# A gated attention mix on one core: the maxima task of row block 0 moves from the last A group of a slot into the second group of the next slot

## The chip, the cores and the metric

The kernel runs on one core of one Trainium2 chip. The metric is the time of one execution on the device, in microseconds (us). The time before is the median of three executions.

Engine names in the rows: PE is the matmul engine (TensorE) and PEld its weight loads, DVE is VectorE, ACT is ScalarE, POOL is GpSimd, and SP is the engine that issues most DMAs.

## The reference

One input `x` (2048 x 512) goes through two attention blocks with 32 heads of 16 dimensions. Block A is causal within each of four segments of 512 rows, and mixes in a running memory state per head; block B is full attention over 2048 rows. A gate per row mixes the two.

```python
def _A_ref(x, wq, wk, wv, wo, beta):          # H = 32, Dh = 16, N = 4 segments, L = 512
    ...
    for s in range(N):
        logits = einsum("bhqd,bhkd->bhqk", qs, ks) * scale + mask     # causal inside the segment
        p = _softmax(logits, axis=-1)
        a_dot = einsum("bhqk,bhkd->bhqd", p, vs)
        ...                                                           # a_mem from the state of the segments before
        o = g * a_mem + (1.0 - g) * a_dot
    return o @ wo

def _B_ref(x, wqkv, wo):
    scores = einsum("bhqd,bhkd->bhqk", q, k) * (Dh ** -0.5)
    p = _softmax(scores, axis=-1)
    return einsum("bhqk,bhkd->bhqd", p, v) @ wo

g = _sigmoid((x * gate_w).sum(-1, keepdims=True))
return g * _A_ref(...) + (1 - g) * _B_ref(...)
```

## The kernel before

The work of a unit is four heads and 512 query rows. There are 32 units of block A (numbered 0 to 31) and 32 of block B (32 to 63). After a first part with the projections, the main loop has 32 slots; slot k computes B's unit `ub` = 32 + k and A's unit `ua` = k.

**Two passes over the scores.** The softmax needs the row maxima before the exponentials. The first pass computes scores with the queries on the partitions and reduces them on VectorE: `s_b` (L467) is one such maxima task of B, two matmuls into a pair of PSUM banks and one reduction of 128 x 1024; `s_a` (L442) is one of A, with causal masks added by small matmuls from `crows` and `cmask`. The pairs of banks, `SBK[0]` and `SBK[1]`, take turns in the order in which the tasks are issued. `m_chain` (L480) makes the negated maxima out of both units' results, and `m_rows` (L503) puts them as extra rows into the query tiles, so that the second pass yields scores less their maximum. A's maxima of unit u go into the chain u + 1, which `m_chain` takes in group 21 of slot u.

**Groups.** The second pass computes the scores transposed, in groups. A slot has 37 groups: 32 for B and then 5 for A. `t_group` (L522) issues the two halves of a group's score matmuls into two of three banks (`tb0`, `tb1`, `mb`); between the two halves it runs the tasks that the plan gives to that group (`between`), for groups of A behind them. ScalarE then writes the exponentials into `raw`. In A's groups GpSimd cuts them to the causal triangle (L546).

**Probability times value.** `pv` (L549) accumulates the product with the values, with a column of ones for the sum, in the bank `PVB`. `pvs` (L866) sets which product comes with which group: group 0 has A's last key block of the slot before, followed by `fin_copy` (L562), in which VectorE copies `PVB` out; group 1 has none; from group 2 on come B's; A's last group has its key blocks 1 and 3.

**The plan.** All is issued in an order written out by hand; each engine takes its instructions in that order. `plan` maps (slot, group) to a list of tasks. B's maxima tasks are spread one to a group. A's six, in the order `ST_A` = (3, 0), (3, 1), (2, 0), (2, 1), (1, None), (0, None), go to the five A groups of the slot before the one that uses them: row block 3 in two halves in the first two, both halves of row block 2 in the third, row block 1 in the fourth, and row block 0 in the fifth, A's last group.

From slot 9 to slot 31, `extras` (L888) puts one output matmul block of 12 matmuls (`out_mm`, L625) ahead of group 2, in group 1.

Of the kernel before, what the change touches and what calls it, by code (L numbers as in the profile page):

```python
# [23 lines left out]
NT = SEQ // 128  # L24
# [10 lines left out]
def gated_mix_kernel(ctx, tc, xt, wq, wk, wv, wo, beta, wqkv, wob, gate_w, out):  # L35
# [635 lines left out]
    def todo(fn, *a):  # L671
        return lambda: fn(*a)
# [90 lines left out]
    for blk in range(16):  # L763
# [9 lines left out]
        n = blk + 1 + (c == 2)  # L773
# [156 lines left out]
    plan = {}  # L930

    def spread(tasks, gs):
        for n, p in enumerate(gs):
            plan.setdefault(p, []).extend(tasks[len(tasks) * n // len(gs):len(tasks) * (n + 1) // len(gs)])

    for k in range(31):
        if k:
            spread([todo(s_b, 33 + k, *t) for t in (sorted(ST_B, key=lambda t: t[2]) if k == 1 else ST_B)],
                   [(k - 1, n) for n in range(2 * S_FIRST, 2 * NT)] + [(k, n) for n in range(2 * S_LAST)])
        else:  # L940
            spread(st33[EARLY:], sorted([(0, n) for n in range(2 * S_LAST)] + [(0, 2 * n) for n in range(4)]))
        for n, t in enumerate(ST_A):
            plan.setdefault((k, 2 * NT + n - (n > 2)), []).append(todo(s_a, k + 1, *t))

    for k in range(32):
        ua, ub = k, 32 + k
# [89 lines left out]
```

## Time and profile before

| | |
|---|---|
| median of three runs | 1942.11 us (1941.66 to 2304.19) |
| the profiled execution | 1943.65 us, span 1941.9 us |
| busy: PE, DVE, ACT, POOL | 99%, 83%, 74%, 16% of the span |
| mean granted TensorE clock | 0.997 |
| slots 1, 2, 4, 5 | about 47.4 us each |
| slots 9 to 29 | about 49.4 us each |

The span reaches from the first to the last instruction; the execution's time has 1.75 us around it. In the rows of a timeline the first number is the start and the second the duration, in us; then come the engine, the line, the operation, output and inputs with their sizes, and the number of instructions merged in the row. In brackets stands the idle time of the engine before it and what ended it. The end of a matmul is modelled, so two matmuls that follow each other can overlap in the rows. Rows that group instructions give count, busy time, mean ns of one, and the idle time before them.

### The profile page before, as it was taken

The page shows a single profiled execution, that of the slowest core. Times are in us where ns is not written, and L with a number is a line of the kernel's source. Part 1 is how long each engine was busy: PE and PEld are TensorE (multiplying, and loading weights), DVE is VectorE, ACT ScalarE, POOL GpSimd, SP SyncE. Part 2 cuts the span into 40 slices and gives each one's busy share as a digit, 9 for nine tenths or more (in the row PEclk, how much of TensorE's full clock was granted, in tenths as well). Part 3 has the DMA queues.
Part 4 walks back from the last instruction along what each step waited for, and adds up shares of the span by engine and source line. Part 5 has one row for each costly group of instructions (what it writes and reads, how often), then busy time and mean ns, then how long its engine had stood idle before and what let it go on. Part 6 is the DMA issues. An engine that isn't in the chain of part 4 may idle for free.

```text
span 1941.9 us, 43661 instructions
## 1 busy us (share of the span) xinstructions
PE 1918.9 (99%) x17485; PEld 927.4 (48%) x17485; DVE 1619.4 (83%) x1678; ACT 1434.8 (74%) x2699; POOL 317.4 (16%) x665
## 2 busy tenths in 40 slices
PE   7999999999999999999999999999999999999999
PEld 5887777444344444444444444444444444444445
DVE  6135766899999999999999999999999999999942
ACT  4233333688888888888888888888888888888884
POOL 5200000011211111111121212121112121212122
PEclk9999999999999999999999999999999999999999
DMA  7666566744443444453435354544445443434111
GB/s 216 165 203 189 188 197 178 174 99 116 99 116 90 105 88 105 87 116 88 115 86 115 87 115 88 116 88 106 94 93 111 93 106 89 106 88 110 49 49 58
DMA packets 163791, 222.50 MB, mean 115 GB/s; under 512 B 39916, under 2 KB 90556, under 8 KB 157828
## 3 DMA queue, kind: packets, MB, share of 16 engines
q1 hardware_dynamic: 159284, 211.41, 44.0%
q0 software_dynamic: 3248, 8.03, 2.2%
q8 instruction: 138, 2.26, 0.5%
q14 instruction: 65, 0.53, 0.1%
q10 hardware_dynamic: 1056, 0.26, 0.1%
HBM read 147.95 MB, written 68.16 MB: 111 GB/s over the span
## 4 chain that ended last, share of the span: by engine, by line
PE 96%; DVE 2%; DMA 0%; ACT 0%; SPq 0%; issue 0%; DVEq 0%; ACTq 0%
PE pvb L559 33%; PE tb L537 18%; PE sbk L474 12%; PE mb L537 9%; PE tb L304 5%; PE sbk L452 3%; PE tb L629 2%; PE mb L304 2%; PE sbk L287 1%; PE tb L287 1%; PE pvb L304 1%; PE mb L629 1%; PE sbk L456 1%; PE mb L287 1%; PE pvb L287 1%; DVE mxb L476 1%
## 5 line engine op out<-in xcount | busy, mean ns | idle before, releaser
L476 DVE TENSOR_REDUCE mxb<-sbk 128x2 f32<-128x1024 f32 x1024 | 1233.2, 1221 | 61.5 <-PE tb L537 30.6
L543 ACT ACTIVATE raw<-tb 128x512 f32<-128x512 f32 x1555 | 887.6, 598 | 146.0 <-PE tb L537 101.8
L559 PE MATMUL pvb<-raw,vb 128*17 128x256 f32 (+1 forms) x8072 | 639.9, 388 | 0.0
L543 ACT ACTIVATE raw<-mb 128x512 f32<-128x512 f32 x782 | 467.6, 598 | 71.2 <-PE mb L537 44.9
L474 PE MATMUL sbk<-xh,qb 64*128 64x512 f32 x1344 | 479.8, 445 | 3.8 <-DVE mxb L476 1.8
L537 PE MATMUL tb<-qb,xh 64*128 64x512 f32 x872 | 352.2, 443 | 0.0
L559 PEld LDWEIGHTS pvb<-raw,vb 128*17 128x17 f32 x8072 | 134.9, 95 | 341.3 <-issue 335.9
L474 PE MATMUL sbk<-kb,qb 64*128 64x512 f32 x704 | 242.1, 444 | 0.0
L537 PEld LDWEIGHTS tb<-qb,xh 64*128 64x128 f32 x872 | 145.9, 185 | 176.6 <-issue 89.7
L537 PE MATMUL mb<-qb,xh 64*128 64x512 f32 x445 | 198.9, 447 | 0.0
L474 PEld LDWEIGHTS sbk<-xh,qb 64*128 64x128 f32 x1344 | 192.2, 184 | 9.1 <-DVE mxb L476 6.1
L537 PE MATMUL tb<-qb,kb 64*128 64x512 f32 x470 | 191.1, 447 | 0.8 <-DVE st L314 0.8
L546 POOL TENSOR_SCALAR_AFFINE_SELECT raw<-raw 128x256 f32<-128x256 f32 (+1 forms) x320 | 115.8, 362 | 355.9 <-ACT raw L543 348.2
L460 DVE TENSOR_REDUCE mx<-sbk 128x2 f32<-128x768 f32 (+1 forms) x128 | 136.6, 1090 | 23.8 <-PE sbk L456 21.1
L537 PEld LDWEIGHTS mb<-qb,xh 64*128 64x128 f32 x445 | 82.1, 184 | 94.9 <-issue 50.4
L537 PEld LDWEIGHTS tb<-qb,kb 64*128 64x128 f32 x470 | 79.2, 184 | 98.8 <-issue 53.1
L537 PE MATMUL mb<-qb,kb 64*128 64x512 f32 x234 | 104.0, 444 | 0.0
L474 PEld LDWEIGHTS sbk<-kb,qb 64*128 64x128 f32 x704 | 96.8, 184 | 5.2 <-issue 3.5
L559 PE MATMUL pvb<-raw,va 128*17 128x256 f32 (+2 forms) x1280 | 94.7, 384 | 0.8 <-ACT pvs L568 0.8
L452 PE MATMUL sbk<-ka,qa 64*128 64x256 f32 (+3 forms) x512 | 87.9, 358 | 1.3 <-DVE mx L460 0.3
L311 ACT ACTIVATE st<-tb 128x512 fp32r<-128x512 f32 x33 | 19.8, 598 | 81.4 <-DVE phi L310 47.3
L537 PE MATMUL tb<-qa,ka 64*128 64x512 f32 (+3 forms) x339 | 79.5, 372 | 0.0
(291 smaller groups left out, 1832.1 us busy)
## 6 DMA issues: line engine op xcount, KB each, us to landing
xh<-dB SPq DMA_DIRECT2D x38, 512.0 KB
vb<-vdB SPq DMA_DIRECT2D x16, 1088.0 KB
dB<-st SPq DMA_DIRECT2D x64, 256.0 KB
dA<-st SPq DMA_DIRECT2D x64, 256.0 KB
pd<-pvs SPq DMA_DIRECT2D x64, 256.0 KB
kb<-dB SPq DMA_DIRECT2D x22, 512.0 KB
xh<-dB SPq DMA_DIRECT2D x38, 256.0 KB
qb<-dB SPq DMA_DIRECT2D x64, 128.0 KB
```

The source lines that it names most:

```text
L287: nc.tensor.matmul(b, lhs, WV[wi][:, k, :], start=n == 0, stop=n == 11)
L304: nc.tensor.matmul(b, WS[ws][w][wi][:, k, :], (XH, XL)[xi][c][:, k, :], start=n == 0, stop=n == 11)
L311: nc.scalar.activation(st[:, 0], b, AF.Copy)
L452: nc.tensor.matmul(b[:, j, c0:c0 + n], q_of(u)[r, p, i * 128:(i + 1) * 128], k_of(u, p)[r, :n], start=True, stop=False)
L460: nc.vector.tensor_reduce(m[:, :, p, i], b[:, :, :n], axis=AX.X, op=OP.max)
L474: nc.tensor.matmul(b[:, j], q_of(u)[r, p, i * 128:(i + 1) * 128], k_of(u, p)[r, kc * C:(kc + 1) * C], start=True, stop=True)
L476: nc.vector.tensor_reduce(MXB[u][:, :, p, i, kc], b, axis=AX.X, op=OP.max)
L537: nc.tensor.matmul(bs[j][:, c0:c0 + w], k_of(u, h // 2)[r, 128 * it:128 * it + 128], q_of(u)[r, h // 2, q0:], start=True, stop=True)
L543: nc.scalar.activation(pt, bs[j], AF.Exp, scale=SCALE)
L546: nc.gpsimd.affine_select(out=m, in_=m, pattern=[[1, 128]] if n < 2 else [[0, 2], [1, 128]], compare_op=OP.is_ge, fill=0.0, base=0, channe ...
L559: nc.tensor.matmul(PVB[32 * h:32 * h + E + 1, q0 + lo:q0 + hi], vt[:, it, 4 * q + h, :], pt[:, lo:hi], start=it == 0 and lo == 0, stop=it ...
L629: nc.tensor.matmul(b, (AT["oh"], AT["ol"])[oi][:, g, a], (AT["wh"], AT["wl"])[wi][:, g, a], start=n == 0, stop=n == 11)
```

## The change

For slots k = 2 to 7 the sixth task of `ST_A`, row block 0 of unit k + 1 (both pairs of heads), is no longer planned for A's last group of slot k, (k, 36), but for group 1 of slot k + 1. There it stands ahead of B's maxima task of that group, and both are issued between the two halves of the group's scores. The task itself, its operands and the chain that takes its result are the same. Slots 1, 2 and 9 to 31 keep the old place.

```diff
         for n, t in enumerate(ST_A):
-            plan.setdefault((k, 2 * NT + n - (n > 2)), []).append(todo(s_a, k + 1, *t))
+            over = n == 5 and 2 <= k < 8
+            plan.setdefault((k + 1, 1) if over else (k, 2 * NT + n - (n > 2)), []).append(todo(s_a, k + 1, *t))
```

## The prediction

> **What bounds the kernel now.** I read the busy shares first, then the busy time by slot, then one slot boundary engine by engine in order of time.
>
> ```profile
> PE 1918.9 (99%) x17485; PEld 927.4 (48%) x17485; DVE 1619.4 (83%) x1678; ACT 1434.8 (74%) x2699; POOL 317.4 (16%) x665
> 451.05:498.49 47.44, 47.40 (x496) 19.10 (x493) 45.71 (x47) 40.77 (x76) 9.90 (x17) 1.00 0.51 120
> 498.49:547.08 48.59, 47.76 (x498) 19.19 (x494) 46.81 (x47) 40.87 (x76) 7.40 (x15) 1.00 0.42 100
> 547.08:594.49 47.41, 47.38 (x497) 19.14 (x493) 45.68 (x47) 40.77 (x76) 9.91 (x17) 1.00 0.49 117
> 689.56:736.94 47.38, 47.34 (x498) 19.19 (x494) 45.42 (x44) 40.72 (x76) 4.58 (x15) 1.00 0.43 90
> 736.94:784.20 47.26, 47.23 (x496) 19.16 (x492) 45.20 (x42) 40.70 (x77) 7.87 (x20) 1.00 0.50 110
> ```
>
> The first row is the page's; the others are slots 2, 3, 4, 7 and 8 (from:to and length, then busy us of PE, PEld, DVE, ACT, POOL, then the TensorE clock). TensorE is busy in all but some hundredths of a slot, at the full clock, and VectorE in 45.2 to 46.8 of 47.3 to 48.6 us. So TensorE sets the pace and VectorE, 4% below it, is the next to do so. But a modelled busy PE also covers matmuls that run without the partner they normally overlap. That shows only in order of time. The boundary into slot 3, PE alone:
>
> ```profile
> 496.72 0.50 PE L537 MATMUL tb<-qa,ka 64*128 64x256 f32 x4
> 497.06 0.22 PE L452 MATMUL sbk<-ka,qa 64*128 64x128 f32 x2
> ...
> 497.50 1.06 PE L559 MATMUL pvb<-raw,va 128*17 128x384 f32 x16
> 498.49 0.49 PE L537 MATMUL mb<-qb,kb 64*128 64x512 f32 x1
> ...
> 499.15 0.63 PE L559 MATMUL pvb<-raw,va 128*17 128x256 f32 x8
> 499.71 0.50 PE L537 MATMUL tb<-qb,kb 64*128 64x512 f32 x1
> ...
> 500.28 0.40 PE L537 MATMUL tb<-qb,kb 64*128 64x512 f32 x1
> 500.54 0.51 PE L474 MATMUL sbk<-xh,qb 64*128 64x512 f32 x2
> 500.95 0.49 PE L537 MATMUL tb<-qb,kb 64*128 64x512 f32 x1
> 501.37 0.67 PE L559 MATMUL pvb<-raw,vb 128*17 128x256 f32 x8
> 501.98 0.50 PE L537 MATMUL mb<-qb,kb 64*128 64x512 f32 x1
> 502.27 0.50 PE L474 MATMUL sbk<-xh,qb 64*128 64x512 f32 x2
> 502.61 0.39 PE L537 MATMUL tb<-qb,kb 64*128 64x512 f32 x1
> 502.93 0.63 PE L559 MATMUL pvb<-raw,vb 128*17 128x256 f32 x8
> 503.49 0.49 PE L537 MATMUL tb<-qb,kb 64*128 64x512 f32 x1
> ...
> 504.71 0.50 PE L537 MATMUL tb<-qb,kb 64*128 64x512 f32 x1
> ```
>
> Here 496.72 starts A's last group, 498.49 group 0 of slot 3, 499.71 group 1, 500.28 group 2, 501.98 group 3, 503.49 group 4, 504.71 group 5. An undisturbed group takes 1.22 us (503.49 to 504.71). Group 1 has no probability-value step and takes 0.57. Groups 2 and 3 take 1.70 and 1.51: together 0.77 us over the pace. VectorE and GpSimd in the same stretch:
>
> ```profile
> 496.28 2.03 DVE L462 TENSOR_REDUCE mx<-sbk 128x4 f32<-128x1024 f32 x2 [0.23 <-PE sbk L456]
> 499.26 1.23 DVE L476 TENSOR_REDUCE mxb<-sbk 128x2 f32<-128x1024 f32 x1 [0.94 <-PE tb L537]
> 500.40 0.68 DVE L566 COPY pvs<-pvb 128x512 f32<-128x512 f32 x1
> 501.00 4.61 DVE L476 TENSOR_REDUCE mxb<-sbk 128x2 f32<-128x1024 f32 x4
> 496.47 0.90 POOL L546 TENSOR_SCALAR_AFFINE_SELECT raw<-raw 128x256 f32<-128x256 f32 x2 [0.77 <-ACT raw L543]
> ```
>
> The reduction of group 0 ends at 499.26 + 1.23 = 500.49, and the maxima matmuls of group 2, which reuse its pair of banks, start 0.05 later, at 500.54. Group 1's reduction starts at 501.00, behind the copy of the finished output, ends at 501.00 + 1.22 = 502.22 (mean below), and group 3's matmuls start at 502.27. So for three groups VectorE is the bound: PE ran one group short of its pace (group 1) and VectorE had the copy besides. Just before that VectorE sat idle for 0.94 us.
>
> **The change part by part.** Six times (into slots 3 to 8) the maxima of row block 0 leave A's last group and go into group 1 of the next slot, ahead of that group's own maxima. Twelve matmuls (4 scores, 8 masks) and one reduction move; no DMA is issued by the step, and none on SP or POOL is passed by it in its own queue. On PE it moves behind A's last 16 probability-value matmuls and all of group 0; on VectorE it moves behind group 0's reduction and the output copy. Count and sizes of the VectorE work:
>
> ```profile
> L476 DVE TENSOR_REDUCE mxb<-sbk 128x2 f32<-128x1024 f32 x1024 | 1233.2, 1221 | 61.5 <-PE tb L537 30.6 <-PE sbk L474 17.9 <-PE mb L537 12.7
> L462 DVE TENSOR_REDUCE mx<-sbk 128x4 f32<-128x512 f32 x32 | 22.2, 693 | 3.5
> L566 DVE COPY pvs<-pvb 128x512 f32<-128x512 f32 x31 | 21.1, 681 | 1.4 <-PE pvb L559 1.4
> ```
>
> **Removed from the last group.** The moved matmuls run from 497.06 to 497.50: 0.44 us of PE. They stand ahead of the probability-value matmuls, and these need the causal masks that GpSimd puts on the group before: 496.47 + 0.90 = 497.37. With a signal of 0.05 to 0.06 us (the two bank releases above) the last of the four head stacks cannot start before 497.43. It starts at 497.50 now. So the 0.44 us is cover for that wait, and of it I take 0.07 as gained. Bounds: 0 if the signal takes longer, 0.44 if the first three stacks, whose masks are older, carry the time. I take 0.07 because the fourth stack's two passes must follow its own mask whatever the others do.
>
> **Added to group 1.** On PE 0.44 us between the two score matmuls of the group. It costs nothing there, since group 1's own maxima now must wait anyway: their pair of banks is the one that group 0's reduction frees (before the change it was the moved task's, long free). Group 0 starts at 498.42, its reduction at 499.19, which ends at 500.42, so these maxima start at 500.47. PE reaches that point at 499.64 + 0.44 = 500.08, and has 0.39 us to spare. Without that cover it would cost up to 0.44. Queued behind the waiting matmul are group 1's second score matmul, with ScalarE's exponential for it, and all of group 2.
>
> **The bank that is late next.** Group 2's maxima now take the pair of banks which the moved reduction reads. VectorE, in order: group 0's reduction at 499.19, the copy 1.14 later (499.26 to 500.40 in the rows) at 500.33, the moved reduction 0.60 later (500.40 to 501.00) at 500.93, ending 0.69 later at 501.62. Group 2's maxima start 0.05 behind, at 501.67, where they started at 500.54: 1.13 later. From there the rows of before go on: 0.83 to the probability-value matmuls (500.54 to 501.37) and 0.61 more to group 3 (to 501.98), so group 3 starts at 501.67 + 1.44 = 503.11. Its maxima need group 1's reduction, which follows the moved one. One reduction of 0.69 should give way after about 0.61 (the copy of 0.68 does after 0.60), so group 1's runs from 501.54 to 502.76 and frees its banks at 502.81, before 503.11. The wait of 0.29 us in group 3 (502.27 less 501.98) is thus gone, and group 3 takes the plain 1.22: group 4 starts at 504.33 and not 503.49. **+0.84 us per boundary**: 1.13 later in group 2, 0.29 given back in group 3. Behind group 4 VectorE has more slack than before (group 2's reduction would end near 503.9, 0.4 us ahead of need), and the slots are paced by PE to their end, so I carry the 0.84 whole.
>
> Weighed against a rule: the Trainium skill, "VectorE: DVE Perf Modes", section "The DRAIN you can't avoid", says that the next operation does not start until the pipe has emptied, with an exception for operations that are not held. Taken by itself it would start the moved reduction a whole copy, 0.68, behind the copy, and make the loss 0.92 per boundary and 5.5 us in all. The rows disagree: 0.60 from start to start under a copy of 0.68, so this is the exception's case.
>
> **The sum** is 6 x 0.84 = +5.0 us, the six boundaries taken as equal, since the slots quoted at the top differ by some 0.1 us but for slot 3's one event below. Bounds by the last group's term: with a gain of 0, 6 x 0.91 = +5.5; with 0.44, everything up to group 2 comes 0.37 earlier and group 3's maxima still find their bank, 6 x 0.47 = +2.8. The profiled execution took 1943.65 us for a span of 1941.9; it becomes a span of 1946.9 and 1948.7 us. It lies 1.54 us over the median of the runs shown, 1942.11, so on the median I predict **1947.1 us**. Part of that 1.54 is visible: one slot here is longer than its neighbours, by the row
>
> ```profile
> 526.81 1.28 DVE L501 SCALAR_TENSOR_TENSOR m<-mx,mhi 128x32 f32<-128x32 f32 x1
> 526.72 1.33 POOL L616 TENSOR_TENSOR wl<-o,wh 128x512 fp32r<-128x512 f32 x1
> ```
>
> where a tiny VectorE operation lasted as long as the GpSimd subtraction beside it. The DMA that releases that subtraction decides whether they meet, so a run may carry one such 1.1 us more or less.
>
> **The rivals.** *Faster: group 1 as free room on PE.* Group 1 lacks its probability-value step, and the moved matmuls fill it; if then the waits of groups 2 and 3 vanish, 6 x 0.77 = 4.6 us are saved: 1937.5 us. For it speaks slot 9, where 2.95 us of output matmuls stand in group 1 and no later group waits:
>
> ```profile
> 786.09 1.20 PE L629 MATMUL tb<-wh,oh 128*128 128x512 f32 x4
> 789.04 0.50 PE L537 MATMUL tb<-qb,kb 64*128 64x512 f32 x1
> 790.26 0.73 PE L474 MATMUL sbk<-xh,qb 64*128 64x512 f32 x2
> ```
>
> Against it: those give VectorE time and no work, while the moved task brings 0.61 us. It decides from the point where the moved reduction ends before group 2 wants the bank, 499.27 + 0.57 + 0.44 = 500.28 with the full 0.44 gained; it cannot, since the copy in front of it starts at 499.96 at the earliest and the two take 1.29.
>
> *A smaller loss*: the last group does gain its 0.44, as bounded: 1944.9 us. *A larger loss*: nothing is gained there and VectorE's lag reaches group 3 too, so that its 0.29 wait stays: 6 x 1.20 = 7.2, 1949.3 us. For it: reduction and copy are back to back from 499.26 on. Against: 0.30 us of margin at group 3 (503.11 against 502.81).
>
> *Nothing*: a later wait in the slot swallows the delay, or the task stays where it was: 1942.1 us. Against the first the slot rows, with 0.03 to 0.05 us of idle PE outside slot 3; against the second the key in the plan, which names group 1 of the next slot for exactly six values of k.
>
> **How the numbers follow.** Chances: the forecast 0.57, the smaller loss 0.17, the larger 0.12, nothing 0.08, faster 0.06. The likeliest case's own range is 1945.5 to 1949. Smaller and larger loss, and about 1 us of scatter by which the profiled execution and the median differ, widen it to 1942.0 to 1949.8. All cases, the faster one included, lie within 2% (38.8 us, about what a measurement of this kernel can tell from no change): faster by over 2% 0.01, slower by over 2% 0.02, within 0.97; these leave room only for something that no row shows.
>
> **What would show it.** Right: at the boundaries into slots 3 to 8 the first probability-value matmuls of A's last group wait on GpSimd; VectorE runs group 0's reduction, copy, a 0.69 reduction and group 1's without a gap, and its idle time ahead of group 0 is about 1.7 us where it was 0.94; group 2's maxima start 0.05 us behind the end of the 0.69 reduction, about 3.25 us after group 0 starts (2.05 now); groups 1, 2 and 3 sum to 4.7 us (3.78 now), with group 3 at 1.22; slots 1, 2 and from 9 on keep their boundaries. Wrong: group 0 starts 0.3 us or more earlier behind A's last scores, group 3 still waits, or slot lengths beyond the boundary change.

## The result and the profile after

The change makes the kernel slower by 0.19%: the ratio to before is 1.0019, with a 95% interval of 1.0011 to 1.0027, which on the median of before, now 1942.65 us over ten runs, is 3.7 us (2.1 to 5.2). The median after is 1946.57 us, where 1947.1 was predicted. That is little, but the interval, made from nine runs before and ten after, lies wholly above 1. One execution of 2304 us before is left out of the comparison as disturbed.

First the slots as a whole (from:to and length, busy us of PE, PEld, DVE, ACT and POOL, the clock). The first row is slots 2 to 8 together, then slots 3, 4 and 5 of the kernel after; the last is slots 2 to 8 before.

```profile
451.18:786.44 335.26, 332.23 (x3448) 134.04 (x3444) 319.26 (x321) 286.34 (x533) 49.30 (x102) 1.00 0.46 104
498.52:546.56 48.04, 47.53 (x494) 19.13 (x493) 45.71 (x47) 40.95 (x77) 7.33 (x15) 1.00 0.47 101
546.56:594.57 48.01, 47.51 (x494) 19.15 (x494) 45.68 (x47) 40.96 (x77) 9.89 (x16) 1.00 0.49 114
594.57:642.63 48.06, 47.58 (x495) 19.18 (x494) 45.71 (x47) 40.96 (x77) 3.61 (x10) 1.00 0.38 87
```

```profile
451.05:784.20 333.15, 332.11 (x3448) 134.09 (x3444) 320.36 (x321) 285.41 (x533) 49.45 (x102) 1.00 0.46 104
```

The work is the same (PE 332.2 and 332.1 us), the stretch is 2.11 us longer, and each of slots 3 to 5 has half a microsecond of idle PE where slots 2 and 4 to 8 had a few hundredths before the change. The two profiled executions differ by less than six boundaries' worth (3.5 us, below), mainly because the one of before held the chance meeting of VectorE and GpSimd in slot 3, 1.1 us, and the one after does not: `m_chain`'s last step there took 0.19 us. The 0.3 us that are still missing were not traced. The profiled executions of e2, e3, e4, e5 and b1 below hold such a meeting too, with a step of `m_chain` that lasts about 1.3 us in slot 3, and those of e1 and b2 do not; it is one part of the scatter of the times here.

The boundary into slot 3 after the change, PE alone:

```profile
496.86 0.50 PE L537 MATMUL tb<-qa,ka 64*128 64x256 f32 x4
497.29 1.31 PE L559 MATMUL pvb<-raw,va 128*17 128x384 f32 x16
498.52 0.50 PE L537 MATMUL mb<-qb,kb 64*128 64x512 f32 x1
...
499.75 0.50 PE L537 MATMUL tb<-qb,kb 64*128 64x512 f32 x1
499.75 0.32 PE L452 MATMUL sbk<-ka,qa 64*128 64x128 f32 x1
...
500.57 0.50 PE L474 MATMUL sbk<-xh,qb 64*128 64x512 f32 x2
500.91 0.39 PE L537 MATMUL mb<-qb,kb 64*128 64x512 f32 x1
500.91 0.39 PE L537 MATMUL tb<-qb,kb 64*128 64x512 f32 x1
501.77 0.49 PE L474 MATMUL sbk<-xh,qb 64*128 64x512 f32 x2 [0.47 <-DVE mx L462]
502.10 0.39 PE L537 MATMUL tb<-qb,kb 64*128 64x512 f32 x1
502.43 0.62 PE L559 MATMUL pvb<-raw,vb 128*17 128x256 f32 x8
502.98 0.50 PE L537 MATMUL mb<-qb,kb 64*128 64x512 f32 x1
...
504.20 0.50 PE L537 MATMUL tb<-qb,kb 64*128 64x512 f32 x1
```

A's last group starts at 496.86, group 0 at 498.52, group 1 at 499.75, group 2 at 500.91 (the second of the two rows), group 3 at 502.98, group 4 at 504.20. And VectorE and GpSimd beside it:

```profile
496.42 1.23 DVE L462 TENSOR_REDUCE mx<-sbk 128x4 f32<-128x1024 f32 x1 [0.24 <-PE sbk L456]
499.29 1.23 DVE L476 TENSOR_REDUCE mxb<-sbk 128x2 f32<-128x1024 f32 x1 [1.65 <-PE tb L537]
500.43 0.68 DVE L566 COPY pvs<-pvb 128x512 f32<-128x512 f32 x1
501.03 0.68 DVE L462 TENSOR_REDUCE mx<-sbk 128x4 f32<-128x512 f32 x1
501.63 4.61 DVE L476 TENSOR_REDUCE mxb<-sbk 128x2 f32<-128x1024 f32 x4
496.61 0.89 POOL L546 TENSOR_SCALAR_AFFINE_SELECT raw<-raw 128x256 f32<-128x256 f32 x2 [0.78 <-ACT raw L543]
```

VectorE idles 1.65 us ahead of group 0, then runs reduction, copy, moved reduction and group 1's reduction without a gap. The moved one ends at 501.71, and group 2's maxima start 0.06 later, at 501.77, after 0.47 us in which PE did nothing at all. The six boundaries, from start to start, are equal to 0.01 us in their sums and to 0.02 in each term:

| us | last A group | group 0 | 1 | 2 | 3 | sum |
|---|---|---|---|---|---|---|
| before | 1.77 | 1.22 | 0.57 | 1.70 | 1.51 | 6.77 |
| predicted | 1.70 | 1.22 | 3.47 for 1 and 2 together | | 1.22 | 7.61 |
| after | 1.67 | 1.22 | 1.17 | 2.07 | 1.22 | 7.35 |

The loss is 0.58 us per boundary, 3.5 us for six, which agrees with the 3.7 us of the ratio.

### The profile page after: what moved, and what is told of

Its sections match the earlier page's. It is cut to its first block, busy times and chain, and to the rows that moved or that the text cites. A ratio compares the mean times of both kernels' runs of the same rounds, so it can differ in the third digit from the quotient of the medians.

```text
span 1944.0 us, 43661 instructions
## 1 busy us (share of the span) xinstructions
PE 1917.7 (99%) x17485; PEld 926.3 (48%) x17485; DVE 1618.0 (83%) x1678; ACT 1435.7 (74%) x2699; POOL 316.9 (16%) x665
## 4 chain that ended last, share of the span: by engine, by line
PE 95%; DVE 3%; DMA 1%; SPq 0%; issue 0%; ACT 0%; DVEq 0%; ACTq 0%
PE pvb L559 33%; PE tb L537 17%; PE sbk L474 12%; PE mb L537 9%; PE tb L304 5%; PE sbk L452 3%; PE tb L629 2%; PE mb L304 2%; PE sbk L287 1%; PE tb L287 1%; PE pvb L304 1%; PE mb L629 1%; PE sbk L456 1%; PE mb L287 1%; PE pvb L287 1%; DVE mxb L476 1%
```

## Experiments

Two questions: is it VectorE's queue (theory V) or only TensorE's work (theory P) that costs, and what did the moved matmuls do in their old place? The times of one kernel scatter (the 27 runs of before that e1 to e4 are compared with lie between 1937.37 and 1944.90 us), so the boundary's rows decide more sharply than the ratios. Rows are of the boundary into slot 4 where nothing else is said.

**The task in both places** (e1_double):

```diff
-            plan.setdefault((k + 1, 1) if over else (k, 2 * NT + n - (n > 2)), []).append(todo(s_a, k + 1, *t))
+            plan.setdefault((k, 2 * NT + n - (n > 2)), []).append(todo(s_a, k + 1, *t))
+            if over:
+                plan.setdefault((k + 1, 1), []).append(todo(s_a, k + 1, *t))
```

> The moved task stays in A's last group as before AND is done a second time in group 1 of slots 3 to 8 (the result is the same maximum written twice). This is the addition without the removal. Measure: time from the start of A's last group to the start of group 4, 6.77 us before and 7.35 us after the change. Theory V (VectorE's queue: copy, then moved reduction, hold the pair of banks that group 2 wants): the last group is 1.77 us again and groups 0 to 3 take 1.22, 1.17, 2.07, 1.22 as after the change, sum 7.45, so +0.68 us at each of six boundaries, +4.1 us, ratio to before 1.0021. Theory P (what costs is only the 0.44 us of matmuls on TensorE, uncovered in their new place): +0.44 us at each, sum 7.21, +2.6 us, 1.0014, with no wait of group 2 on the moved reduction.

Ratio 1.0015 (1.0006 to 1.0024), which both theories allow. The boundary does not: 1.77, 1.22, 1.17, 2.07, 1.22, sum 7.44, as V said, with the same wait on the moved reduction:

```profile
547.79 0.68 DVE L462 TENSOR_REDUCE mx<-sbk 128x4 f32<-128x512 f32 x1
548.52 0.49 PE L474 MATMUL sbk<-xh,qb 64*128 64x512 f32 x2 [0.47 <-DVE mx L462]
```

So the addition alone costs 0.68 per boundary, and the removal gives back 0.10 of it.

**B's own maxima first** (e2_own_first):

```diff
             mid = plan.pop((k, n)) if n < 2 * NT and (k, n) in plan else []
+            if n == 1 and 3 <= k <= 8:
+                mid = mid[1:] + mid[:1]
```

> As after the change, but in group 1 B's own maxima come first and the moved task behind them. TensorE's work is the same. Theory V: VectorE now runs group 0's reduction, the copy, group 1's reduction (1.22) and then the moved one (0.69), and group 2 takes the banks that group 1's own reduction frees, so group 2's maxima start 0.53 us later than after the change; sum from A's last group to group 4 7.88 us, +1.1 us per boundary against before, +6.7 us, ratio to before 1.0034. Theory P: order is irrelevant, sum 7.35, ratio as after the change, 1.0018 to 1.0019.

Ratio 1.0040 (1.0027 to 1.0052); V's 1.0034 lies in it, P's 1.0018 does not. The sum is 7.86 to 7.89. Group 2 now waits for group 1's long reduction, 549.56 + 1.22 = 550.78:

```profile
549.56 1.22 DVE L476 TENSOR_REDUCE mxb<-sbk 128x2 f32<-128x1024 f32 x1
550.69 0.68 DVE L462 TENSOR_REDUCE mx<-sbk 128x4 f32<-128x512 f32 x1
550.83 0.49 PE L474 MATMUL sbk<-xh,qb 64*128 64x512 f32 x2 [0.80 <-DVE mxb L476]
```

The same matmuls and the same reductions in another order cost 0.52 us more per boundary. TensorE's work alone cannot be the reason.

**The copy on ScalarE** (e3_act_copy, on the kernel after; e4_before_act_copy, on the kernel before):

```diff
-        if u < 31:
+        if u < 31 and not 2 <= u < 8:
             nc.vector.tensor_copy(ps, PVB)
```

> As after the change, but for slots 3 to 8 the copy of A's finished output (fin_copy of units 2 to 7) runs on ScalarE, which has room, and so leaves VectorE's queue. Theory V: the moved reduction starts 0.60 us earlier, group 2's maxima start about 2.65 us after group 0 and not 3.24; sum from A's last group to group 4 between 6.76 us (if what follows group 2's maxima takes 1.21 us to the start of group 3, as after the change) and 6.99 (if 1.44, as before it): -0.1 to +1.3 us against before, ratio 1.0000 to 1.0007. Theory P: sum stays 7.35, ratio 1.0018 to 1.0019.

> The kernel before, with the copy of A's finished output on ScalarE in slots 3 to 8. Theory V: group 1's reduction starts 0.55 us earlier, group 3 no longer waits (1.22 us and not 1.51), group 2 keeps its 1.70 since it waits for group 0's reduction; sum from A's last group to group 4 6.48 us, -0.29 us per boundary, -1.7 us, ratio 0.9991. Theory P: VectorE's queue does not count at the boundary, sum 6.77, ratio 1.0000.

With the change: ratio 1.0006 (0.9997 to 1.0014), sum 6.95, as V said and against P. The moved reduction starts earlier by 0.42 us, not 0.60, measured from group 0: at 2.09 (547.20 less 545.11) where it was 2.51 (501.03 less 498.52). VectorE would be free at 547.01, 1.14 behind group 0's reduction; what is late then is PE, whose last moved matmuls end at 546.94 + 0.23 = 547.17. So group 2's maxima start 2.84 us after group 0 (547.95 less 545.11), where 2.65 was expected.

```profile
545.11 0.49 PE L537 MATMUL mb<-qb,xh 64*128 64x512 f32 x1
546.94 0.23 PE L456 MATMUL sbk<-cmask,crows 64*128 64x64 bf16 x2
547.15 0.50 PE L474 MATMUL sbk<-xh,qb 64*128 64x512 f32 x2
545.87 1.23 DVE L476 TENSOR_REDUCE mxb<-sbk 128x2 f32<-128x1024 f32 x1 [1.65 <-PE tb L537]
547.20 0.69 DVE L462 TENSOR_REDUCE mx<-sbk 128x4 f32<-128x512 f32 x1
547.95 0.49 PE L474 MATMUL sbk<-xh,qb 64*128 64x512 f32 x2
```

Without the change: ratio 1.0004 (0.9994 to 1.0014), where 0.9991 was expected, a miss. Group 3 did lose its wait (1.22), but group 2 grew from 1.70 to 1.89, and the sum is 6.67 and not 6.48. Six times 0.10 us less than before lies inside the interval, so the times do not show a gain. The reason for the longer group 2 is ScalarE: the copy stands in front of group 1's exponentials, the first of these ends at 549.45 + 0.62 = 550.07, and group 2's second score matmul, which needs its bank, starts 0.05 later.

```profile
548.97 0.60 ACT L568 ACTIVATE pvs<-pvb 128x512 f32<-128x512 f32 x1
549.45 0.62 ACT L543 ACTIVATE raw<-tb 128x512 f32<-128x512 f32 x1
550.12 0.49 PE L537 MATMUL tb<-qb,xh 64*128 64x512 f32 x1
```

**The task in group 8** (e5_group8):

```diff
-            plan.setdefault((k + 1, 1) if over else ...
+            plan.setdefault((k + 1, 8) if over else ...
```

> The moved task goes into group 8 of slots 3 to 8 and not into group 1. This is the removal alone at the boundary, with the addition where VectorE has caught up. Theory V plus cover (the 0.44 us of matmuls were cover for the wait on GpSimd's masks in A's last group, so that taking them away gives back only 0.10): A's last group 1.67, groups 0 to 3 as before the change (1.22, 0.57, 1.70, 1.51, sum with the last group 6.67), group 8 about 1.66 and not 1.22, groups 9 and 10 unmoved at 1.22: +0.34 us per slot, +2.0 us, ratio to before 1.0010. Rival (the place is all that matters, and VectorE's idle time makes the task free anywhere else): -0.10 per slot, -0.6 us, 0.9997. Rival P: 0.44 us wherever it lies, and nothing given back by the last group: +2.6 us, 1.0014.

Ratio 1.0021 (1.0012 to 1.0031); the forecast of 1.0010 was too low. At the boundary it held: the last group takes 1.67, groups 0 to 3 as before. It failed in group 8, which takes 2.05 and not 1.66:

```profile
559.64 0.50 PE L537 MATMUL tb<-qb,xh 64*128 64x512 f32 x1
559.65 0.32 PE L452 MATMUL sbk<-ka,qa 64*128 64x128 f32 x1
559.88 0.31 PE L452 MATMUL sbk<-ka,qa 64*128 64x128 f32 x2
560.11 0.30 PE L452 MATMUL sbk<-ka,qa 64*128 64x128 f32 x1
560.26 0.23 PE L456 MATMUL sbk<-cmask,crows 64*128 64x64 bf16 x2
560.48 0.50 PE L474 MATMUL sbk<-xh,qb 64*128 64x512 f32 x2
561.69 0.49 PE L537 MATMUL mb<-qb,xh 64*128 64x512 f32 x1
556.82 3.60 DVE L476 TENSOR_REDUCE mxb<-sbk 128x2 f32<-128x1024 f32 x3
```

The group's own maxima start 0.83 us behind the first moved matmul (560.48 less 559.65), where 0.44 was expected. Two things hold them, and they end within 0.1 us of each other. On PE the moved matmuls of one half of the rows come behind the group's first score matmul, so the halves run one after the other (the rows of 1, 2 and 1 matmuls): from the first to the last masks it is 0.61 us, against 0.28 in the last group before (497.06 to 497.34). There the next matmuls came 0.16 behind these masks, at 497.50; here that would be 560.42. And the moved task has taken a turn of the banks, so that the group's own maxima need the banks of group 7's reduction, which ends at 556.82 + 3.60 = 560.42, 0.06 before they start. A quicker passage on PE would have gained next to nothing. The forecast had counted only the 0.44 us and left this wait out.

The boundary sum minus 0.10 and the 0.83 make +0.73 per slot, 4.4 us, in line with the ratio. So away from the boundary the move loses as well: two maxima tasks in one group make the second wait for the reduction of the group before. The task was cheap in its old place.

**The other direction** (b1_group0_early, b2_group1_early), on the kernel before, for slots 1 to 8; b2 has `(k, 1)` for `(k, 0)`:

```diff
+    for k in range(1, 9):
+        plan.setdefault((k - 1, NG - 1), []).extend(plan.pop((k, 0)))
```

> The kernel before with a move in the other direction: B's maxima task of group 0 of slots 1 to 8 goes forward into A's last group of the slot before, behind row block 0's task, into VectorE's idle 0.94 us. Theory V: the copy follows directly on the probability-value matmuls of group 0, group 2's maxima find their banks free, and ScalarE or group 1's reduction holds groups 2 and 3 by some 0.2 us. Last group about 2.17 us, group 0 0.89, group 1 0.57, group 2 about 1.4, group 3 1.22 to 1.4, sum 6.3 against 6.77: -0.45 us at each of eight boundaries, -3.6 us, ratio to before 0.9981. Theory P (nothing but TensorE's work counts): sum 6.77 to 6.9, ratio 1.0000 to 1.0005.

> The same with group 1's maxima task of slots 1 to 8 (group 0 keeps its own). Theory V: group 2's maxima find their banks free, but the copy still stands behind group 0's reduction, so group 2's probability-value matmuls wait for the copy by some 0.4 us. Last group about 2.17 us, group 0 1.22, group 1 0.34, group 2 about 1.6, group 3 1.22, sum 6.59 against 6.77: -0.18 us at each of eight boundaries, -1.4 us, ratio to before 0.9993. Theory P: sum 6.77 to 6.9, ratio 1.0000 to 1.0005.

Both missed. b1: ratio 1.0007 (0.9997 to 1.0017), boundary 2.25, 0.98, 0.69, 1.58, 1.22, sum 6.72, only 0.05 under before. b2: ratio 1.0008 (0.9998 to 1.0018), boundary 2.25, 1.22, 0.45, 1.82, 1.22, sum 6.96. Of b1's 0.4 us over the forecast the largest part, 0.18, is in group 2, and 0.08 to 0.12 each in the last group and groups 0 and 1. For the part in group 2: in b1 VectorE now waits for work and no matmul of group 2 waits for it, yet group 2 is late, for ScalarE's exponentials of groups 0 and 1 come one after the other:

```profile
547.62 0.69 DVE L566 COPY pvs<-pvb 128x512 f32<-128x512 f32 x1 [0.71 <-ACT raw L543]
546.98 0.60 ACT L543 ACTIVATE raw<-mb 128x512 f32<-128x512 f32 x1 [1.10 <-PE tb L537]
547.47 1.15 ACT L543 ACTIVATE raw<-tb 128x512 f32<-128x512 f32 x2
548.67 0.50 PE L537 MATMUL tb<-qb,xh 64*128 64x512 f32 x1
```

The second score matmul of group 2 (548.67) starts 0.05 behind the end of the third exponential (547.47 + 1.15 = 548.62). In b2 too group 2's second score matmul starts 0.05 us behind the end of an exponential (549.60; 548.95 + 0.60 = 549.55), and not behind the copy, as was expected. And the task itself costs 0.48 us in the last group (2.25 less 1.77). So three engines stand within some tenths of a microsecond of each other at this boundary: part of what VectorE gives up, ScalarE takes. None of these versions is measurably faster than the kernel before; e4 and b1 have a boundary that is shorter by 0.10 and 0.05 us, too little for their intervals to show.

## Why the prediction was right

**Who sets the pace, and where.** Right. VectorE's queue bounds groups 2 and 3 of a boundary, and e2 and e3 move the time by changing its order and its load.

**The last group** (gain of 0.07 out of 0.44, the rest cover for GpSimd's masks). Right: 0.10, and e1 and e5 give the same 0.10. The first three head stacks now start at 497.29 without a wait, so the sign that "the first probability-value matmuls of A's last group wait on GpSimd" is not met as it was worded: the fourth alone waits. Its masks end at 496.61 + 0.89 = 497.50, and it starts 0.05 behind them, at 497.56:

```profile
497.56 0.11 PEld L559 LDWEIGHTS pvb<-raw,va 128*17 128x17 f32 x2
```

That is 0.70 us after the last group's start (496.86). In the kernel before all four stacks started together and the fourth at 497.52, 0.80 after it, 0.15 behind the end of its masks. The older stacks carried nothing: the group ends as much earlier as the fourth starts earlier.

**The moved matmuls in group 1** (no cost, 0.39 us of cover to spare). Right that they cost nothing of their own, since group 1's maxima wait until 500.57, just behind group 0's reduction (499.29 + 1.23 = 500.52). The margin was wrong: the last masks start at 500.36, 0.61 us after the first of the moved matmuls, where the old place took 0.28 us for the same, so PE is ready at about the time when the banks come free. It would have mattered without VectorE's wait: in e3 they are what is late.

**The bank of group 2.** Right to 0.01: its maxima start 3.25 us after group 0 (501.77 less 498.52), as forecast, and group 3's wait is gone.

**What follows group 2's maxima** is the term that was mis-sized. I took 0.83 + 0.61 = 1.44 us from the rows of before to the start of group 3; it took 502.98 less 501.77 = 1.21. In the kernel before ScalarE held this stretch, which the prediction left out. These are its rows there:

```profile
500.30 0.60 ACT L543 ACTIVATE raw<-tb 128x512 f32<-128x512 f32 x1 [0.20 <-PE tb L537]
500.80 0.59 ACT L543 ACTIVATE raw<-mb 128x512 f32<-128x512 f32 x1
```

Group 2's second score matmul started at 500.95, 0.05 after the first of them ended, and 0.41 behind the maxima. The product of the fourth head, which needs the second, started 0.05 behind its end (500.80 + 0.59 = 501.39):

```profile
501.44 0.11 PEld L559 LDWEIGHTS pvb<-raw,vb 128*17 128x17 f32 x2
```

After the change group 2 waits for VectorE so long that ScalarE's part has passed. The second score matmul follows the maxima by 0.33 us, 0.08 less. From the probability-value matmuls to group 3 it takes 0.55 and not 0.61. The other 0.09 lie between these two: the probability-value matmuls follow a score matmul that had to wait by 0.42 us (500.95 to 501.37), and one that runs on directly by 0.33 (502.10 to 502.43). So 0.23 us of the new wait overlapped an old one. The other runs agree: from group 2's maxima to group 3 it is 1.22 us in e1 and e3, where the maxima are late too, and 1.63 in e4 (549.51 to 551.14), where ScalarE has the copy besides. With the 0.23 and the last group's 0.10 for 0.07 the step of 0.84 becomes 0.58, and the sum 3.5 us and not 5.0.

**The number.** The forecast time of 1947.1 us is nearer to the measured 1946.57 than the forecast step to the measured one, and that is luck: the median of before moved up from 1942.11 to 1942.65 with more runs and made up for part of the 1.3 us by which the step of 5.0 was too large. The 2% that the prediction took for the least a measurement can tell was far too much: the interval here is 0.16% wide.

**The rivals.** *Faster* is out by the interval: group 3 lost its wait of 0.29 us, but groups 1 and 2 grew by 0.97. *The larger loss* is out, since group 3 runs at 1.22. *Nothing* is out by the interval. *The smaller loss*, 2.8 us, is near the measured size, but its reason is not the one: the last group gave 0.10, not 0.44.

**The rule on the drain.** The Trainium skill, "VectorE: DVE Perf Modes", section "The DRAIN you can't avoid", would have had the moved reduction start a full copy behind the copy. It started 0.60 us behind a copy of 0.68 (500.43 and 501.03), and the next reduction 0.60 behind one of 0.68 (501.03 and 501.63): again the exception that the section names.

## What to carry to other kernels

Ask of a task not only how long it runs but what it covers: 0.44 us of matmuls at a place where the engine would have waited anyway cost about 0.10 us, and 0.83 in the middle of a dense group, where it also took another task's turn of the banks. A reduction put behind a copy in a queue delays whoever next needs its bank, so count the queue from the last common event to the release. And when a wait grows, look for the other waits it now hides before adding it up: here 0.23 us per boundary came from ScalarE's exponentials and was paid already.

## What the runs showed that was not expected

Small matmuls between the two score matmuls of a group take longer on TensorE than behind a finished pair: from the first of the twelve to the last masks it was 0.61 us in group 8 of e5 and in group 1 after the change, and 0.28 in A's last group before. ScalarE, 74% busy over the kernel, binds at the slot boundary: in e4, b1 and b2 a score matmul starts 0.05 us after an exponential releases its bank, and in e4 this takes back 0.19 of the 0.29 us that VectorE's relief gave.
